# A written engine order for a decode step of attention and a gated MLP: q's copies first, softmax in front of GLU work, scores in two tiles

## Chip, cores, metric

The kernel runs on one core of one Trainium2 chip. The metric is the device time of one execution in microseconds (us). A profile's span is some 2.2 us shorter than the time of the same execution (81.6 against 83.79 in the profiled run of the kernel before). Some executions come out over 1.5% slower than the fastest of the same kernel; they are called slow, and only the other, fast runs are compared.

## The reference

One token, bf16. A 32-head attention with 8 key/value heads over the last 4096 positions of a cache, and a gated MLP of width 1792, mixed by a scalar gate g:

```python
q = (x @ wq)                                  # wq 512 x 4096
scores = einsum("bhqd,bhkd->bhqk", q, k) * Dh ** -0.5      # k, v: 8 heads x 4096 x 128
p = softmax(scores); o = einsum("bhqk,bhkd->bhqd", p, v)
a = o.reshape(1, 1, 4096) @ wo                # wo 4096 x 512
h = sigmoid(x @ w_gate) * (x @ w_up)          # 512 x 1792 each
b = h @ w_down
return g * a + (1 - g) * b                    # g = sigmoid(sum(x * gate_w))
```

Every weight and cache row is used once. The work is to move 30.67 MB and to keep the engines out of the way.

## The kernel before

One queue loads the weights and the cache in this order: wq, four pairs of key heads (kn), w_gate, w_up, four pairs of value heads (vv), w_down (wd), wo; the last pair of value heads comes in two halves, with half of wd behind each. The tile framework puts the instructions of an engine in an order of its own; the text below is not the order in which they ran. "PV" is the product of probabilities and values. In the code and the views qtT and qbig are q transposed and laid out as weights, kT the transposed keys, S_ps the scores, pm and hm their maxima, e_sb and eT the exponentials and their transpose, pv_ps the result of PV, a_ps the sum of the output row; `down()` adds rows of the product with wd to it.

```python
for k in range(8):                                   # q, broadcast over the partitions
    ...  nc.tensor.matmul(q_ps[:], lhsT=xT[...], rhs=wq_sb[:, c, ks], ...)
    nc.scalar.copy(q_sb[:, ks], q_ps[:])
    if k % 2: nc.vector.transpose(qtT..., q_sb...)
for qd in range(4):                                  # q into block-diagonal weights
    for t in range(2):
        nc.vector.tensor_copy(q_dst[rows, :, 32*qd:32*qd+R2, :, t], q_src[rows, :, :, :, 0, t])

S_ps = ps_S.tile([P, 4, 512], F32, name="S_ps", tag="S")        # one tile of 4 banks
for a in range(HP):                                  # 4 pairs of key heads
    for v in range(2):
        kT = ktp.tile(...); nc.vector.transpose(kT..., kn[a]...)
        ...  nc.tensor.matmul(S_ps[:, 2*v+hb, :], lhsT=q_st..., rhs=k_v..., start=False, ...)   # 8

for v in range(2): nc.vector.tensor_reduce(pm2[:, v:v+1], S_ps[:, 2*v:2*v+2, :]..., op=ALU.max)
nc.vector.tensor_tensor(pm[:], pm2[:, 0:1], pm2[:, 1:2], op=ALU.max)
...  # mt = pm^T (TensorE), hm = max over heads (VectorE), mb = hm^T (TensorE), nb (ScalarE)
for v in range(2):
    nc.scalar.activation(e_sb[:, v, :], S_ps..., AF.Exp, bias=nb[:], ..., accum_out=rs2[:, v:v+1])
    nc.vector.transpose(eT..., e_sb[:, v, :]...)
...  # GLU: gate and up products, sge = exp(-gate), sge+1, sg = 1/sge, h_sb, hT (VectorE)
...  # lsel, rb_ps, rb: 1/sum of the exponentials
for a in range(HP):
    for m in range(NP // 4):
        if a == HP - 1 and m == NP // 8: down(0, NJ_A)
        nc.tensor.matmul(pv_ps[32*a:32*a+32, :, :], lhsT=eT..., rhs=vv[a][:, 4*m:4*m+4, :], ...)
...  # o_ps, oT, oX, oY, the rest of down()
for c in range(NC_O):                                # wo, in six loads of 8, 8, 8, 5, 2, 1 chunks
    add_row(oY[:, c:c+1], wo_sb[:, c, :], False, c == NC_O - 1)      # two products of 256 columns
```

## Time and profile before

| | before |
|---|---|
| time, median of three runs | 84.48 us (84.08 to 84.76) |
| span of the profiled run | 81.6 us |
| TensorE / VectorE / ScalarE busy | 51.6 / 38.6 / 10.1 us |
| loads | 30.67 MB, 376 GB/s over the span |

In the page's rows of slices each digit is the busy share of one fortieth of the span in tenths (9 is 90% or more); PEclk is the clock granted to TensorE. In lines of chain and timeline the first number is the start in us, the second the length; a bracket at the end of a timeline line tells how long the engine stood idle before and what ended it. The prediction below shows these views.

### The profile page before, as it was taken

The numbers are of one execution on the slowest core, as the hardware profiler recorded it, in microseconds if no ns is written. First come the engines' busy times: TensorE is split into PE (matmuls) and PEld (weight loads), VectorE is DVE, ScalarE is ACT, GpSimd is POOL, SyncE is SP. The second block draws the span as 40 slices with busy tenths as digits, with TensorE's granted clock in tenths as the row PEclk, the third lists the DMA queues.
The fourth block names the chain that finished last, engine by engine and source line by source line (L and its number), as shares of the span: only waits on it lengthen the run. The fifth ranks groups of instructions, "written<-read, shape, count | busy, mean of one in ns | idle before, by whom it ended". The sixth has DMA issues, their size and how long they took to land.

```text
span 81.6 us, 791 instructions
## 1 busy us (share of the span) xinstructions
PE 51.6 (63%) x313; PEld 24.0 (29%) x313; DVE 38.6 (47%) x50; ACT 10.1 (12%) x18; POOL 3.3 (4%) x10
## 2 busy tenths in 40 slices
PE   0200286999400499999999063300999999967960
PEld 0200122344000233444443033000433444545830
DVE  0601820034999999999903995699300000002020
ACT  2300000376500000000000200910000000020010
POOL 7800000000000000000000000000000000000000
PEclk9999999999998555999999997555555999999999
DMA  5969969999999999999999999999999999995000
GB/s 161 353 289 482 514 273 490 393 418 474 401 426 458 410 434 425 436 422 412 421 422 458 410 426 450 409 426 391 417 428 420 420 422 422 424 399 217 0 0 1
DMA packets 3050, 30.71 MB, mean 376 GB/s; under 512 B 356, under 2 KB 616, under 8 KB 1128
## 3 DMA queue, kind: packets, MB, share of 16 engines
q1 hardware_dynamic: 3042, 30.67, 89.7%
q8 instruction: 2, 0.03, 0.2%
q10 hardware_dynamic: 6, 0.00, 0.0%
HBM read 30.67 MB, written 0.00 MB: 376 GB/s over the span
## 4 chain that ended last, share of the span: by engine, by line
PE 55%; DVE 24%; DMA 15%; ACT 1%; issue 1%
PE S_ps L215 20%; PE pv_ps L304 17%; DMA wq_sb<-in_A_wq_dram 15%; PE q_ps L184 8%; PE a_ps L290 6%; DVE kT L209 5%; DVE sg L266 4%; DVE pm L222 3%; DVE eT L242 3%; DVE h_sb L268 3%; DVE qbig L197 2%; DVE qtT L189 2%; PE o_ps L313 1%; PE gu_ps L255 1%; DVE hT L273 1%
## 5 line engine op out<-in xcount | busy, mean ns | idle before, releaser
L215 PE MATMUL S_ps<-kT,qbig 128*128 128x512 bf16 x64 | 16.6, 424 | 6.2 <-DVE qbig L197 6.2
L209 DVE STREAM_TRANSPOSE kT<-kn 128x2048 f32<-128x2048 f32 x8 | 17.8, 2275 | 0.0
L304 PE MATMUL pv_ps<-vv,eT 128*32 128x512 bf16 x64 | 14.2, 436 | 0.0
L215 PEld LDWEIGHTS <-qbig 128*128 128x128 bf16 x64 | 6.7, 106 | 16.1 <-DVE qbig L197 7.0
L184 PE MATMUL q_ps<-wq_sb,xT 128*128 128x512 bf16 x32 | 8.4, 428 | 1.0 <-DMA wq_sb<-in_A_wq_dram 1.0
L304 PEld LDWEIGHTS <-eT 128*32 128x32 bf16 x64 | 5.8, 109 | 7.6 <-issue 3.6
L315 DVE TENSOR_TENSOR oT<-o_ps,rb 128x32 bf16<-128x32 f32 x1 | 0.2, 191 | 15.2 <-PE o_ps L313 15.2
L189 DVE STREAM_TRANSPOSE qtT<-q_sb 128x512 f32<-128x512 f32 x4 | 2.8, 702 | 7.5 <-ACT q_sb L186 7.5
L203 PE MATMUL S_ps<-ident,other 2*128 2x512 bf16 x4 | 2.0, 611 | 5.8 <-DVE other L141 5.8
L186 ACT CAST q_sb<-q_ps 128x512 bf16<-128x512 f32 x8 | 4.7, 585 | 6.5 <-PE q_ps L184 6.5
L184 PEld LDWEIGHTS <-xT 128*128 128x128 bf16 x32 | 3.4, 108 | 6.4 <-issue 3.7
L279 PE MATMUL rb_ps<-lsel,ones_f 128*128 128x32 f32 x2 | 0.6, 398 | 5.6 <-DVE lsel L277 5.6
L222 DVE TENSOR_REDUCE pm<-S_ps 128x1 f32<-128x1024 f32 x2 | 2.4, 1219 | 3.2 <-PE S_ps L215 3.2
L290 PE MATMUL a_ps<-wo_sb,oY 128*1 128x256 bf16 x64 | 3.7, 272 | 0.0
L263 ACT ACTIVATE sge<-gu_ps 128x448 f32<-128x448 f32 x1 | 0.5, 543 | 23.1 <-PE gu_ps L258 23.1
L290 PEld LDWEIGHTS <-oY 128*1 128x1 bf16 x64 | 2.8, 84 | 0.7
L266 DVE RECIPROCAL sg<-sge 128x448 f32<-128x448 f32 x1 | 3.0, 2954 | 0.0
L309 ACT COPY pv_sb<-pv_ps 128x512 f32<-128x512 f32 x1 | 0.6, 586 | 18.7 <-PE pv_ps L304 18.7
L268 DVE SCALAR_TENSOR_TENSOR h_sb<-gu_ps,gg,sg 128x448 bf16<-128x448 f32 x1 | 2.2, 2154 | 1.5 <-PE gu_ps L255 1.5
L166 DVE TENSOR_TENSOR gpr<-xr 1x512 f32<-1x512 bf16 x1 | 0.7, 679 | 4.6 <-DMA xr<-in_gate_w_dram 4.6
L149 PE MATMUL xt_ps<-ident,xr 1*128 1x1 bf16 x4 | 0.3, 166 | 3.5 <-POOL ident L130 3.5
L203 PEld LDWEIGHTS <-other 2*128 2x128 bf16 x4 | 0.6, 158 | 6.2 <-DVE other L141 5.9
(60 smaller groups left out, 32.5 us busy)
## 6 DMA issues: line engine op xcount, KB each, us to landing
kn<-in_A_k_cache_dram SPq DMA_DIRECT2D x4, 2048.0 KB, 27.2
vv<-in_A_v_cache_dram SPq DMA_DIRECT2D x3, 2048.0 KB, 19.1
wq_sb<-in_A_wq_dram SPq DMA_DIRECT2D x1, 4096.0 KB
wo_sb<-in_A_wo_dram SPq DMA_DIRECT2D x3, 1024.0 KB, 22.9
vv<-in_A_v_cache_dram SPq DMA_DIRECT2D x2, 1024.0 KB
wg_sb<-in_B_w_gate_dram SPq DMA_DIRECT2D x1, 1792.0 KB, 32.9
wd_sb<-in_B_w_down_dram SPq DMA_DIRECT2D x2, 896.0 KB
wu_sb<-in_B_w_up_dram SPq DMA_DIRECT2D x1, 1568.0 KB
```

The source lines that it names most:

```text
L184: nc.tensor.matmul(q_ps[:], lhsT=xT[:, c:c + 1].to_broadcast([P, P]), rhs=wq_sb[:, c, ks], start=(c == 0), stop=(c == DC - 1))
L186: nc.scalar.copy(q_sb[:, ks], q_ps[:])
L189: nc.vector.transpose(qtT[:].bitcast(F32)[:, kq], q_sb[:].bitcast(F32)[:, kq])
L203: nc.tensor.matmul(S_ps[:, u, :], lhsT=other[:].rearrange("p o y u -> p (o y u)"), rhs=ident[0:2, 0:2].rearrange("p (o y) -> p o y", o=1). ...
L209: nc.vector.transpose(kT[:].bitcast(F32), kn[a][:, v * KB:(v + 1) * KB, :] .rearrange("p n d -> p (n d)").bitcast(F32))
L215: nc.tensor.matmul(S_ps[:, 2 * v + hb, :], lhsT=q_st[:, a, dhi, :, t], rhs=k_v[:, hb * 16:(hb + 1) * 16, dhi, :, t], start=False, stop=(a ...
L222: nc.vector.tensor_reduce(pm2[:, v:v + 1], S_ps[:, 2 * v:2 * v + 2, :].rearrange("p a b -> p (a b)"), axis=AX.X, op=ALU.max)
L242: nc.vector.transpose(eT[:, :, v * KB:(v + 1) * KB, :].rearrange("p a n r -> p n a r"), e_sb[:, v, :].rearrange("p (n a r) -> p n a r", a= ...
L266: nc.vector.reciprocal(sg[:], sge[:])
L268: nc.vector.scalar_tensor_tensor(h_sb[:].rearrange("p j i -> p i j"), gu_ps[1][:, 0:FQ].rearrange("p (i j) -> p i j", j=NJ), gg[:, 1:2], s ...
L290: nc.tensor.matmul(a_ps[32 * i:32 * i + 1, i, 0:HN], lhsT=lhsT, rhs=rhs[:, i * HN:(i + 1) * HN], start=start, stop=stop)
L304: nc.tensor.matmul(pv_ps[32 * a:32 * a + 32, :, :], lhsT=eT[:, a, 4 * m:4 * m + 4, :].rearrange("p n r -> p (n r)"), rhs=vv[a][:, 4 * m:4 ...
```

## The change

The intent is to shorten the compute chain, which ends last. From q on TensorE, VectorE and ScalarE run in the order of the text. (1) q's copies go in front of the second key transpose, and two of the eight go to ScalarE. (2) The softmax chain goes in front of the GLU's VectorE work, and the inverse sums leave the path to PV. (3) The scores get two tiles, so that the first maximum need not wait for the last product. The core of the diff:

```diff
+    ctx.enter_context(tc.manual_schedule(engines=ORDERED))     # TensorE, VectorE, ScalarE
+    S_ps = [ps_S.tile([P, 2, 512], F32, name="S_ps", tag="S") for _ in range(2)]
...
     for k in range(8):
...
+        if k == 1:
+            kTs[0, 0] = k_transpose(0, 0)
...
-            nc.vector.tensor_copy(q_dst[rows, :, 32 * qd:32 * qd + R2, :, t], q_src[rows, :, :, :, 0, t])
+            copy = nc.scalar.copy if qd == 3 else nc.vector.tensor_copy
+            copy(q_dst[rows, :, 32 * qd:32 * qd + R2, :, t], q_src[rows, :, :, :, 0, t])
...
-    S_ps = ps_S.tile([P, 4, 512], F32, name="S_ps", tag="S")
...
+    glu(0, wg_sb)                     # gate products behind the scores
+    sge = ...; nc.scalar.activation(sge[:], gu_ps[0][:, 0:FQ], AF.Exp, scale=-1.0)
     mt_ps = ...                       # mt, hm, mb, nb as before
+    glu(1, wu_sb)                     # up products beside the exponentials
     for v in range(2): ...            # exponentials, transposes
+    lsel = ...                        # then sge+1, reciprocal, h_sb, hT (moved here)
...
+        if a == 0:                    # rb behind the first quarter of PV
+            nc.tensor.matmul(rb_ps[:], lhsT=ones_f[:], rhs=lsel[:], start=True, stop=True)
```

## The prediction

> **What bounds the kernel now.** I read the page's row of slices first, then the chain that ended last, then that chain in order of time, and last the traffic of the loads near the end.
>
> The slices of the page of the kernel before (40 slices of 2.04 us each):
>
> ```profile
> PE   0200286999400499999999063300999999967960
> DVE  0601820034999999999903995699300000002020
> PEclk9999999999998555999999997555555999999999
> DMA  5969969999999999999999999999999999995000
> GB/s 161 353 289 482 514 273 490 393 418 474 401 426 458 410 434 425 436 422 412 421 422 458 410 426 450 409 426 391 417 428 420 420 422 422 424 399 217 0 0 1
> ```
>
> Two things run side by side. The loads are busy from the seventh slice to the 36th without a gap, at 390 to 490 GB/s. TensorE has two holes, one before the scores (slices 11 to 13) and one in the softmax (slices 22 to 28), and a half clock after each hole.
>
> The chain that ended last, in order of time (start, length, what):
>
> ```profile
> 0.73 12.16 DMA wq_sb<-in_A_wq_dram
> ...
> 25.95 0.32 DVE qbig L197 x2
> ...
> 27.56 16.58 PE S_ps L215 x64
> 44.14 0.02 issue
> 44.16 2.36 DVE pm L222 x2
> 46.52 0.30 DVE sge L264
> 46.82 0.07 DVE pm L225
> 46.89 2.92 DVE sg L266
> 49.81 0.14 DVE hm L229
> ...
> 57.30 0.61 PE rb_ps L279 x2
> 57.91 11.63 PE pv_ps L304 x52
> ...
> 74.47 4.40 PE a_ps L290 x78
> 78.87 0.40 DVE res L330
> ```
>
> So the end is set by compute: wq lands, q, key transposes in front of q's copies, scores 27.56 to 44.14, 13.8 us from there to the first PV product, 14 us of PV, tail. In the softmax, VectorE does the GLU's reciprocal (2.92 us) between the maximum and the step (hm) that TensorE waits for, and later h_sb (2.15) and hT (0.65) before the transposes of the exponentials.
>
> How near behind is the load stream? Windows of the kernel before near the end (last column GB/s, the one before it the load share):
>
> ```profile
> 74.50:75.00 0.50, 0.50 (x12) 0.40 (x10) 0.19 (x1) 0.00 (x0) 0.00 (x0) 1.00 0.62 221
> 75.00:75.50 0.50, 0.50 (x15) 0.39 (x12) 0.00 (x0) 0.00 (x0) 0.00 (x0) 1.00 0.15 49
> 75.50:76.00 0.50, 0.50 (x14) 0.41 (x10) 0.00 (x0) 0.00 (x0) 0.00 (x0) 1.00 0.00 0
> ```
>
> The last byte, the tail of wo, arrives at about 75.45 us of a span of 81.6. TensorE then still works through wo until 78.87, and from there to the end are 2.73 us. The output needs all of wo, so loads are a second bound, only about 3 us behind the first. **This is the number that decides the prediction.**
>
> **What the skill says.** "Perfetto Trace Analysis", Roofline, gives some 435 GB/s as what one core's 16 DMA engines can carry together; the trace agrees (421 to 435 GB/s over every stretch of several us from 12.9 to 72), so no order of compute can hurry the stream. "TensorE: Matmul & The Clock Gate", What's actually happening: after an idle window of about 3.4 us the clock halves, and a busy window of that length brings it back. The trace agrees: after each hole the clock row shows 5, and weight loads of the scores and of PV come 0.427 us apart at first, about 0.22 later. The same page, Architectural detail, says ScalarE and VectorE are strict first-in first-out. That is why a GLU reciprocal in the wrong place costs the chain its whole length, as seen above (hm starts at 49.81, the moment sg ends, though its product was ready near 47.4). "ScalarE: Activation LUTs", What ACT_TABLE_LOAD costs, gives 186 ns + 0.833 ns per element with immediate scale: 239 ns for the moved copies of 64 elements (an estimate from that page; the same formula gives 612 ns for the q copies of 512, where the trace has 585).
>
> **The change part by part.**
>
> 1. q's copies first. VectorE has now two key transposes (2.19 us each of chain) between qtT and qbig. One (0,0) moves into the wait for q: the first kn lands at about 17.7 (cumulated traffic of 4.19 + 2.10 MB), so it runs about 17.8 to 20.1. Then three qtT of 0.71; the last waits for the cast that ended at 21.95 and is done at about 22.7. Six copies instead of eight on VectorE at 1.77/8 = 0.22 each: 24.0. ScalarE does the other two beside them (2 x 0.24). Scores start at 24.0 instead of 27.56: **3.5 us earlier**.
>
> 2. Scores. Seven transposes remain from 24.0, at 2.21 us each back to back (13.28/6): last done at 39.5. Before, TensorE was the slower one here (64 products, the first dozen at half clock, 16.58 us). Now VectorE is: a block of 8 products takes 8 x 0.22 = 1.7 us at full clock. Last block ends at 39.5 + 1.75 = 41.3, so 2.85 us earlier than 44.14; 0.7 of the 3.5 are lost to VectorE.
>
> 3. Scores in two tiles. Before, the maximum of the first half waited for all 64 products (both reductions start after 44.14). Now the first (1.2 us) can run from 39.5 while the last block multiplies; only the second is exposed: 41.3 + 1.22 + 0.15 = 42.7. **1.2 us.**
>
> 4. Softmax chain in front of GLU work. TensorE: gate products (16 in 0.94 us) 41.3 to 42.3, hidden beside the second reduction; mt 0.3, hm 0.22 + 0.24, mb 0.58, nb 0.17, with gaps 44.4. Exponentials 1.1 each with an accumulator read: 45.7 and 46.8; transposes 1.13 each behind them: 46.8 and 47.95. The up products (0.95 us) hide behind the exponentials. rs and lsel 0.4 are no longer in front of PV, since the sum's product is written after the first quarter of PV. **PV starts at about 48.0 instead of 57.84: 9.8 us earlier in all.** add, reciprocal, h_sb, hT (0.38 + 2.95 + 2.15 + 0.65 = 6.1 us) end near 54.6, long before their first use.
>
> 5. PV then meets the data. By cumulated traffic the four vv land at about 45.7, 50.7, 55.5 and 62.6, wd's halves at 60.0 and 64.7, and wo's pieces at 67.2, 69.7, 72.8, 74.45, 75.1 and 75.45. PV from 48.0: 16 products are 3.4 us at full clock, 6.8 at half. With one slow start: 54, 57.6, 61, and the last half after 62.6 ends at 65.3. Copy, o_ps, oT, oX, oY take 2.4 us as before: wo could start at 68 and catches up with its second piece. About 2 us of slack remain against the stream, more because the small last pieces come late.
>
> 6. The end. Last wo piece: 75.45, plus 0.38 from last byte to first product (as wq: last byte near 12.56, product at 12.94) = 75.83. Waiting for pieces, TensorE is busy under half of the time (8 chunks warm = 0.9 of 2.45 us), so I expect half clock at the end. Then five chunks landing at 74.83 take 5 x 0.213 = 1.07, the next two 0.43, the last 0.21 with a drain: ends at 76.7. At full clock it is 76.2. Plus 2.73 from last product to end: span **78.95 (warm) to 79.45 (cold)**, against 81.6. The gain is 2.15 to 2.65 us, a quarter of the 9.8 us won on the compute chain.
>
> **Rivals.**
>
> A. No second bound in the way: the end moves with PV, 9.8 us earlier, some 74.7 us. Against it: wo's last byte at 75.45 and a stream already at its ceiling. The stream could end earlier only if it had waited for buffers; vv waits for key tiles, but the queue shows only 0.4 us of wait on the key transposes and no dip in the row, and the stream has deep work queued. I give this 2%.
>
> B. The written order stalls an engine: VectorE's early key transpose stands in front of three qtT, and a late kn would push q; or TensorE waits in gate, up or wd products in front of something ready. The loads of the GLU weights land by 41, before use; kn at 17.7 is close to the wish (17.5), so slips of 0.3 us are likely and cost nothing because part 5 has 2 us of slack. A stall of 4 us would bring "same": 83 to 84.5. 5%.
>
> C. The stream itself: the timed runs may load 1% slower than the profiled one. Before feels this only through wq (0.1 us), the new kernel feels all of it (0.75 us): 82.7. With that the verdict comes to the 2% line (82.79). This is the main way to "same".
>
> D. A colder end, with wo's earlier pieces also not caught up: at half clock each big piece takes 1.7 us, less than the 2.45 between landings, so the backlog is bounded, at most 0.5 us: 82.5.
>
> **Range.** From the median, 84.48 - 2.45 = 82.0 (before to after by spans, nearer the middle of warm and cold). C and D on one side, an overlap better by some 0.9 us on the other: 81.1 to 83.1. The line of 2% is 0.8 us above my value, against an uncertainty of about 0.6 in the middle: 0.83 faster, 0.16 same, 0.01 slower.
>
> **What will show it.** Scores begin near 24 and VectorE has no gap from 24 to 39.5; the first reduction overlaps the last products; hm directly follows mt; PV begins near 48; TensorE shows holes between wo products from 69 to 75.5 that end with wo's landing; the chain that ended last names the load of wo (or a queue of loads) instead of PV; traffic still stops near 75.4; last product to end still 2.7 us. I am wrong if traffic stops clearly earlier or later than 75.4, or if PV ends after 70, so that the compute chain stays the bound.

## The result

The changed kernel took 81.61 us (median of four fast runs, 81.31 to 82.08) against 84.41 us for the kernel before (84.08 to 84.76, four runs). The ratio is 0.967 with a 95% interval of 0.961 to 0.973. A ratio is the mean time of one kernel's fast runs over that of the other's fast runs of the same rounds, so it is not quite the ratio of the medians. Five further rounds on a chip used later gave 0.982 (0.974 to 0.990): the gain is 2 to 3%, and its size depends on something that the experiments come to.

The page of the changed kernel:

```profile
PE   0200194999914788898887547999998488724550
DVE  0601820029859999999986349999300000200020
PEclk9999999999999999999999995699999999999997
DMA  6789898999999999999999999999999999999600
GB/s 166 281 347 529 363 429 380 438 438 438 421 429 438 429 421 432 412 448 415 411 434 438 413 438 429 438 413 405 411 423 433 406 432 405 417 425 403 245 6 1
...
DMA 90%; SPq 4%; PE 2%; DVE 1%; issue 0%
DMA wg_sb<-in_B_w_gate_dram 42%; DMA vv<-in_A_v_cache_dram 25%; DMA wo_sb<-in_A_wo_dram 23%; SPq L85 3%; PE a_ps L300 2%; SPq L81 1%; DVE res L346 1%
```

The hole before the scores is short and the hole in the softmax nearly gone, yet TensorE is half idle or more near the end (slices 36 to 39). The loads run without a gap into the 38th slice (75.4 us), about as long as before. The chain that ended last is loads for 90% of the span. Before it was TensorE and VectorE.

The compute chain of the changed kernel, in order of time:

```profile
23.48 1.35 DVE L218 COPY qbig<-qtT 32x64 bf16<-32x64 bf16 x6
23.54 0.76 ACT L218 COPY qbig<-qtT 32x64 bf16<-32x64 bf16 x2 [0.84 <-DVE qtT L207]
24.84 1.89 PE L229 MATMUL S_ps<-kT,qbig 128*128 128x512 bf16 x8 [2.76 <-DVE qbig L218]
24.86 15.47 DVE L190 STREAM_TRANSPOSE kT<-kn 128x2048 f32<-128x2048 f32 x7
...
40.26 1.18 DVE L251 TENSOR_REDUCE pm<-S_ps 128x1 f32<-128x1024 f32 x1
...
42.32 1.23 DVE L251 TENSOR_REDUCE pm<-S_ps 128x1 f32<-128x1024 f32 x1 [0.88 <-PE S_ps L229]
...
44.30 0.28 DVE L260 TENSOR_REDUCE hm<-mt_ps 1x32 f32<-1x128 f32 x1 [0.56 <-PE mt_ps L258]
...
48.06 5.13 PE L315 MATMUL pv_ps<-vv,eT 128*32 128x512 bf16 x16 [1.43 <-DVE eT L274]
```

The scores start 2.7 us earlier than before, one reduction lies beside products, hm follows the maximum with no GLU work in between, and PV starts at 48.06 instead of 57.84. Then the products of wo, and the traffic near the end (last column GB/s):

```profile
68.77 1.04 PE L300 MATMUL a_ps<-wo_sb,oY 128*1 128x256 bf16 x16 [0.20 <-DMA wo_sb<-in_A_wo_dram]
71.26 1.04 PE L300 MATMUL a_ps<-wo_sb,oY 128*1 128x256 bf16 x16 [1.46 <-DMA wo_sb<-in_A_wo_dram]
73.75 1.04 PE L300 MATMUL a_ps<-wo_sb,oY 128*1 128x256 bf16 x16 [1.45 <-DMA wo_sb<-in_A_wo_dram]
75.33 1.26 PE L300 MATMUL a_ps<-wo_sb,oY 128*1 128x256 bf16 x16 [0.55 <-DMA wo_sb<-in_A_wo_dram]
```

```profile
75.00:75.50 0.50, 0.17 (x4) 0.14 (x5) 0.00 (x0) 0.00 (x0) 0.00 (x0) 1.00 0.19 68
75.50:76.00 0.50, 0.50 (x12) 0.30 (x10) 0.00 (x0) 0.00 (x0) 0.00 (x0) 1.00 0.05 16
```

Each of the three big pieces of wo is waited for and used up before the next is there; the products of the three small ones (the last line) run together. The last packet of wo's last piece (the only 128 packets of 1024 bytes in that stretch) ends at 75.84 us, where the kernel before had it at 75.45. The last product ends at 76.60, and 2.78 us later the span is over.

### The profile page after: what moved, and what is told of

The parts are those of the page before. It is cut to its first block, busy times and chain, and to the rows that moved or that the text cites. A ratio compares the mean times of both kernels' runs of the same rounds, so it can differ in the third digit from the quotient of the medians.

```text
span 79.4 us, 799 instructions
## 1 busy us (share of the span) xinstructions
PE 52.4 (66%) x313; PEld 23.2 (29%) x313; DVE 38.6 (49%) x48; ACT 10.9 (14%) x20; POOL 3.3 (4%) x10
## 4 chain that ended last, share of the span: by engine, by line
DMA 90%; SPq 4%; PE 2%; DVE 1%; issue 0%
DMA wg_sb<-in_B_w_gate_dram 42%; DMA vv<-in_A_v_cache_dram 25%; DMA wo_sb<-in_A_wo_dram 23%; SPq L85 3%; PE a_ps L300 2%; SPq L81 1%; DVE res L346 1%
## 5 line engine op out<-in xcount | busy, mean ns | idle before, releaser
L229 PE MATMUL S_ps<-kT,qbig 128*128 128x512 bf16 x64 | 15.2, 377 | 5.0 <-DVE qbig L218 2.8
L315 PE MATMUL pv_ps<-vv,eT 128*32 128x512 bf16 x64 | 14.8, 408 | 2.9 <-DMA vv<-in_A_v_cache_dram 1.5
L229 PEld LDWEIGHTS <-qbig 128*128 128x128 bf16 x64 | 6.1, 97 | 14.1 <-issue 4.2
L202 PE MATMUL q_ps<-wq_sb,xT 128*128 128x512 bf16 x32 | 9.0, 451 | 1.4 <-DMA wq_sb<-in_A_wq_dram 1.4
L300 PE MATMUL a_ps<-wo_sb,oY 128*1 128x256 bf16 x64 | 4.4, 272 | 3.6 <-DMA wo_sb<-in_A_wo_dram 3.6
L274 DVE STREAM_TRANSPOSE eT<-e_sb 128x1024 bf16<-128x1024 bf16 x2 | 2.4, 1224 | 1.9 <-ACT e_sb L272 1.9
L300 PE MATMUL a_ps<-wd_sb,hT 128*1 128x256 bf16 x28 | 2.2, 271 | 0.6 <-DMA wd_sb<-in_B_w_down_dram 0.6
```

What stands on the lines that cost most here:

```text
L202: nc.tensor.matmul(q_ps[:], lhsT=xT[:, c:c + 1].to_broadcast([P, P]), rhs=wq_sb[:, c, ks], start=(c == 0), stop=(c == DC - 1))
L229: nc.tensor.matmul(S_ps[v][:, hb, :], lhsT=q_st[:, a, dhi, :, t], rhs=k_v[:, hb * 16:(hb + 1) * 16, dhi, :, t], start=False, stop=(a == HP ...
L274: nc.vector.transpose(eT[:, :, v * KB:(v + 1) * KB, :].rearrange("p a n r -> p n a r"), e_sb[:, v, :].rearrange("p (n a r) -> p n a r", a= ...
L300: nc.tensor.matmul(a_ps[32 * i:32 * i + 1, i, 0:HN], lhsT=lhsT, rhs=rhs[:, i * HN:(i + 1) * HN], start=start, stop=stop)
L315: nc.tensor.matmul(pv_ps[32 * a:32 * a + 32, :, :], lhsT=eT[:, a, 4 * m:4 * m + 4, :].rearrange("p n r -> p (n r)"), rhs=vv[a][:, 4 * m:4 ...
```

## The experiments

A call is a set of runs on one chip. All outputs passed the comparison with the reference. Two kernels compute a wrong result on purpose and passed as well, so the comparison is too coarse to see that part of wo; it says nothing of their correctness.

### Half of wo, in both kernels

The first pair asks which kernel the loads bind: 2.1 MB less to load, the same products.

```diff
-    WO_SPLIT = (0, 8, 16, 24, 29, 31, 32)
+    WO_SPLIT = (0, 8, 13, 15, 16)
-        add_row(oY[:, c:c + 1], wo_sb[:, c, :], False, c == NC_O - 1)
+        add_row(oY[:, c:c + 1], wo_sb[:, c % 16, :], False, c == NC_O - 1)
```

In the kernel before:

> The kernel before with only half of wo loaded, each loaded piece used twice (wrong result on purpose): 2.1 MB less, the same products. Theory (before, the compute chain set the end): the stream ends near 70.5 us instead of 75.45, and the span stays at 81.6 +- 0.4. Rival (the stream bound the kernel before too): the span falls by up to 4.9 us.

In the changed kernel:

> The changed kernel with the same half of wo (wrong result on purpose). Theory (the last byte of wo sets the end): the stream ends near 71 us; TensorE has oY near 68.5 and 64 products of wo left, half of which wait for nothing after the stream's end, so the last product is near 73.1 and the span near 75.9, 3.5 us less than 79.4. Rival (the changed kernel is still bound by PV): span stays at 79.4 within 0.5.

Before: ratio 0.998 (0.989 to 1.007), span 81.5, though its last byte came at 70.68, 4.8 us earlier. Changed: ratio to the kernel before 0.934 (0.928 to 0.939), span 76.1, last byte at 70.84. The products of wo, first of the kernel before with half of wo, then of the changed kernel with half of wo:

```profile
75.12 3.66 PE L290 MATMUL a_ps<-wo_sb,oY 128*1 128x256 bf16 x64
```

```profile
70.33 3.01 PE L300 MATMUL a_ps<-wo_sb,oY 128*1 128x256 bf16 x48 [0.54 <-DMA wo_sb<-in_A_wo_dram]
```

The same cut is worth nothing before and 3.3 us after (spans of 79.4 and 76.1; the whole changed kernel had not run in this call, and the ratio fell from 0.967 in the first result to 0.934). So the bound changed from compute to the stream: shown, not only argued.

### A longer softmax chain

The second pair asks how far ahead of the stream the compute chain runs. One reciprocal, or three, are put between the maximum and hm:

```diff
     glu(0, wg_sb)
+    for _ in range(1):                      # 3 in the second kernel
+        nc.vector.reciprocal(pad[:], pad[:])     # 128 x 448, result unused
```

> The changed kernel with one more VectorE reciprocal of 128x448 (2.95 us) between the maximum and hm, in the middle of the softmax chain, its result unused. It lengthens the chain by about 2.4 us (VectorE idles 0.56 there already): PV starts near 50.5. Theory (PV runs ahead of the data by about 5.7 us, summed from TensorE's waits for vv, wd and wo): span unchanged, 79.4 +- 0.4. Rival (chain still bounds the end): 81.8.

> The same with three of the reciprocals: the chain is 8.3 us longer, PV starts near 56.4. Theory: some 5.7 us are swallowed by the slack, the rest shows: span about 82, between 81.3 and 83.5, depending on the granted clock after a longer hole. Rival (chain still bounds): 87.7. Rival (much more slack than I count): 79.4.

The profiled run with one was slow; its three fast runs had a mean of 81.83 us, ratio 0.978 (0.970 to 0.985), on a chip where the changed kernel itself had not run. Again beside the changed kernel:

> The changed kernel itself, as the anchor for the other three of this call on one chip. Span 79.4 to 80.9: the last byte of wo came at 75.5 to 76.7 us in the runs so far, whatever the compute did, and the span is that plus 3.5 to 4.2.

> delay_1 again beside its anchor, since its profiled run was of the slow state and its fast runs lay 1% over what I expected from another chip. Theory (2.5 us longer softmax chain lies in the slack): same as the anchor within 0.5 us, TensorE still waits for wo's pieces. Rival (part of the chain's length reaches the end): 1 to 2.4 us slower than the anchor.

The changed kernel as anchor had 82.23 us (mean of five fast runs, 81.72 to 82.85) and a span of 79.9; with one reciprocal 81.69 us (six, 81.35 to 81.88), span 79.9. With one reciprocal:

```profile
50.06 5.32 PE L319 MATMUL pv_ps<-vv,eT 128*32 128x512 bf16 x16 [0.31 <-DVE eT L278]
...
73.64 3.45 PE L304 MATMUL a_ps<-wo_sb,oY 128*1 128x256 bf16 x32 [1.46 <-DMA wo_sb<-in_A_wo_dram]
```

PV starts 1.5 us later than in the anchor of the same chip (48.52; I had expected 2.4, but its q was quicker) and TensorE still waits 1.46 us for a piece of wo: the time has not grown. With three, PV starts at 56.7, and no product of wo waits for anything:

```profile
74.74 3.66 PE L304 MATMUL a_ps<-wo_sb,oY 128*1 128x256 bf16 x64
```

Its span is 81.5, ratio 1.002 (0.995 to 1.010). A chain 8.6 us longer (56.7 against 48.06) ends 1.8 us later (78.40 against 76.60), so some 6.8 us were swallowed; I had counted 5.7. The two profiles are of different calls.

### Each part alone

If the end is a floor at the stream, any part that shortens the chain by over some 2 us should reach it. Part 2 alone puts back parts 1 and 3:

```diff
-        if k == 1:
+        if k == 5:
             kTs[0, 0] = k_transpose(0, 0)
+    kTs[0, 1] = k_transpose(0, 1)
-            copy = nc.scalar.copy if qd == 3 else nc.vector.tensor_copy
-            copy(q_dst...
+            nc.vector.tensor_copy(q_dst...
-    S_ps = [ps_S.tile([P, 2, 512], ...) for _ in range(2)]
+    S_all = ps_S.tile([P, 4, 512], F32, name="S_ps", tag="S")
```

> The changed kernel with the softmax chain in front of the GLU work, but q's copies behind two key transposes and all on VectorE as before, and the scores in one tile as before. Chain: scores end near 44.2, PV starts near 51 instead of 48. Theory (stream bounds, 5.7 us of slack): span 79.4, the same as the whole change within 0.4, so this part alone is worth all of the gain. Rival (every part adds to the end): about 81.6 - 2.3*0.6 = 80.2 or later.

Measured: ratio 0.975 (0.968 to 0.982), between the two values of the whole change; span 79.6. The kernel with part 2 alone:

```profile
51.72 6.42 PE L316 MATMUL pv_ps<-vv,eT 128*32 128x512 bf16 x16 [1.43 <-DVE eT L275]
...
75.55 1.27 PE L301 MATMUL a_ps<-wo_sb,oY 128*1 128x256 bf16 x16 [0.53 <-DMA wo_sb<-in_A_wo_dram]
```

PV starts 3.7 us later than with the whole change and the end is the same, with wo waited for. No gain of parts 1 and 3 on top of part 2 shows within the intervals.

Part 1 alone, and none of the three:

> The changed kernel with q's copies first alone: the GLU's add, reciprocal, h_sb and hT are put back in front of hm and of the exponentials' transposes, the sum's product in front of PV, the scores in one tile. Chain: scores end near 42.2, PV starts near 56, about 2 us earlier than the kernel before. Theory: the end moves with the chain until it meets the stream: span 79.4 to 79.9, since 81.6 - 2 is just at the stream's 79.4. Rival (only the softmax order matters): 81.6.

> All three parts put back, only the written order itself kept (the kernel before's order written down by hand, as its trace shows it). Both theories: span 81.6 +- 0.5, PV from 57.8: same as before. If it differs, something of the change that I do not name (the written order itself) moves the time.

Both came out slower than I expected: 0.983 (0.974 to 0.991) and 1.012 (1.002 to 1.022). I had written the old softmax order down wrongly: the up products stood behind mb, and from the end of the scores to PV it took 15.5 us in both kernels, where the kernel before took 13.7. So the second is no control for the written order itself, and what that order is worth alone stays untested. Against each other the two do say something: the ratio with part 1 is lower by 0.03, from three fast runs of each (three of the first kernel's six runs were slow). PV starts at 57.90 in the one and at 60.73 in the other, but this second profile is of a slow run. With the up products back in front of hm:

```diff
+    glu(1, wu_sb)
     hm = work.tile([1, 4, HQ], F32, name="hm")
...
-    glu(1, wu_sb)
     h_sb = work.tile([P, NJ, 32], BF16, name="h_sb")
```

> q's copies first alone, now with the up products in front of the second small softmax product as the kernel before ran them (my first version had them behind it and its softmax took 15.5 us instead of 13.7). PV starts near 56, so the chain alone would end near 79.0. Theory: end at the stream's floor, within 0.5 us of the anchor. Rival (the softmax order is needed): 1 us or more slower than the anchor.

Measured: ratio 0.971 (0.964 to 0.977), mean of five fast runs 81.27 us (81.00 to 81.43), span 79.3. **This is 1.0 us less than the whole change on the same chip** (82.23, of which the fastest run is 81.72), and it beats both kernels. My rival, that the softmax order is needed, falls; but a gain over the anchor I had not expected either. PV and the last wo products of this kernel, and then those last products of the anchor:

```profile
54.94 10.98 PE L317 MATMUL pv_ps<-vv,eT 128*32 128x512 bf16 x53
...
75.24 1.26 PE L299 MATMUL a_ps<-wo_sb,oY 128*1 128x256 bf16 x16 [0.54 <-DMA wo_sb<-in_A_wo_dram]
```

```profile
73.56 3.58 PE L300 MATMUL a_ps<-wo_sb,oY 128*1 128x256 bf16 x32 [1.45 <-DMA wo_sb<-in_A_wo_dram]
```

The windows of the last 8.5 us (TensorE busy first, then weight loads and the other engines; the third last column is the granted clock), of part 1 alone and of the anchor:

```profile
69.00:72.00 3.00, 2.79 (x35) 2.00 (x37) 0.59 (x3) 0.00 (x0) 0.00 (x0) 1.00 1.01 414
72.00:75.00 3.00, 1.98 (x34) 1.30 (x29) 0.00 (x0) 0.00 (x0) 0.00 (x0) 1.00 0.84 330
```

```profile
69.00:72.00 3.00, 1.56 (x28) 1.05 (x25) 0.00 (x0) 0.00 (x0) 0.00 (x0) 1.00 1.00 415
72.00:75.00 3.00, 1.55 (x18) 0.88 (x15) 0.00 (x0) 0.00 (x0) 0.00 (x0) 0.59 0.86 341
```

And of the whole change in its first profile, that of the result above:

```profile
69.00:72.00 3.00, 1.54 (x30) 1.12 (x26) 0.00 (x0) 0.00 (x0) 0.00 (x0) 1.00 1.00 414
72.00:75.00 3.00, 1.34 (x22) 0.78 (x19) 0.00 (x0) 0.00 (x0) 0.00 (x0) 1.00 0.87 342
```

The stream's last byte came at 75.73 in part 1 alone and at 75.63 in the anchor. From there to the last product it took 0.77 us in the one, at full clock, and 1.51 us in the other, at half clock. The anchor's TensorE had run ahead, stood idle half of the time while it waited for wo, and had lost its clock when the last pieces came. The kernel that starts PV 6.4 us later has hardly any idle time from 69 to 72. But the first profile of the whole change was as idle as the anchor and kept its clock: an idle TensorE can lose it there and need not. That this pair of profiles differs by clock at the end is shown; that the 1.0 us between the timed runs has this cause alone is not, since a run's record has only its mean clock.

On this chip the mean times of the fast runs were, by the start of PV in the profile: 82.23 us (48.5, the anchor), 81.69 (50.1, one reciprocal), 81.65 (51.7, part 2 alone), 81.27 (54.9, part 1 alone), 82.27 (57.9, its first version, in which no product of wo waited). So the earliest PV was not the fastest. The profile of the kernel with one reciprocal has half clock at the end as well (1.36 us from last byte to last product) and the anchor's span, 79.9; what its other, faster runs had at their end is not on record.

### The load of w_up

In the traces sixteen packets are in flight, each followed by the next, so the packets can be put in order into sixteen chains (a reconstruction: the trace does not name the engines). In the changed kernel they end between 73.9 and 75.84 us. The kernel loads the end of w_up in four small loads; I took these for the cause:

```diff
-    dq.dma_start(wu_sb[...][:, 0:LM], ...)      # main part
-    ... dq.dma_start(wx_sb[32 * b:32 * b + 32, h, :], wx_v[h, b])      # 4 loads
+    dq.dma_start(wu_sb[:], B_w_up.rearrange("(p c) f -> p c f", c=DC))
```

> The changed kernel with w_up loaded whole over 128 partitions, in place of a main part and four small loads of 32 partitions. In the traces of both kernels eight of sixteen packet chains carry all the 1792-byte packets, and the chains end between 73.9 and 75.8 us. Theory (the stream's end is set by the most loaded chains): spread evenly, the last byte comes near 75.1 instead of 75.84, the span near 78.7. Rival (the spread at the end has another cause): last byte and span unchanged, 75.8 and 79.4.

It fell. Ratio 0.981 (0.975 to 0.988), no better than the anchor's 0.982; last byte at 76.51. Fourteen chains ended within 0.4 us (74.23 to 74.59), and two late, at 75.95 and 76.51. Two loads of 16 KB on a queue named instruction stood near 39.3 and 65.9 us. At the first, one chain had no packet for 1.1 us and then one of 1.00 instead of 0.54 us. A kernel with fewer TensorE instructions should have one less:

```diff
-        for i in range(2):
-            nc.tensor.matmul(a_ps[32 * i:32 * i + 1, i, 0:HN], lhsT=lhsT, rhs=rhs[:, i * HN:(i + 1) * HN], ...)
+        nc.tensor.matmul(a_ps[0:1, 0, 0:N_OUT], lhsT=lhsT, rhs=rhs, ...)
```

> even_wu with 501 instead of 601 TensorE instructions (rows of wd and wo as one product of 512 columns instead of two of 256, no products for the extra x). In even_wu two loads of the queue named instruction, 16 KB each, near 39 and 66 us, each held one of the sixteen packet chains for 1.1 us, and two chains ended at 76.0 and 76.5 where the other fourteen ended near 74.5. Theory (an instruction load for every 256 instructions of TensorE holds one DMA engine back): one such load instead of two, one late chain instead of two. The end is still set by that one: last byte near 76.2, span 79.5 to 80.3. Rival (the two late chains have another cause): still two late chains, with one load of instructions.

Inconclusive: the kernel still had two of these loads, as the row of its queues says, and two late chains (75.91 and 76.04):

```profile
q8 instruction: 2, 0.03, 0.2%
```

I had taken too few instructions away. The trace has 538 rows of TensorE, control rows included, instead of 634 (I had counted 501 and 601), and in all fourteen profiles the second load comes when TensorE has begun 429 to 472 rows. Ratio 0.982 (0.977 to 0.988), which says little either: the edit also changed the copy and store of the output, and eight chunks of wo took TensorE 1.89 us in it, as eight products, against 1.04 us as sixteen in the other kernels. That late chains and instruction loads belong together fits all of this and is not shown by a kernel with one load. It stays open.

## Why the prediction was right

**The deciding number held.** I put the second bound at the last byte of wo, 75.45 us, and the span 3.5 to 4 us behind it. Measured: 75.84, and 3.54 us. My sign of being wrong, traffic that stops clearly later than 75.4, was 0.4 us off here and up to 1.2 us in the fast profiles of its variants. Time 81.61 against 82.0 predicted. Rival A (the end moves with PV, 9.8 us) is refuted by half of wo and by the reciprocals: most of the 9.8 us won on the chain lies in waits for vv and wo.

**Part by part.** Scores start: 24.84, not 24.0. q took 9.00 us instead of 8.40, its first products at half rate for longer (0.43 us apart, though the PEclk row shows 9 there), and the two copies on ScalarE took about 0.5 us each, not the 0.24 from the page's formula; they still ended before VectorE's (24.30 against 24.83). Scores bound by VectorE: right, seven transposes in 15.47 us without a gap, and TensorE idle 0.3 us in front of each block. First reduction hidden: right (40.26, beside the products that start at 40.39). PV at 48.06, predicted 48.0, but by two errors that cancel: the chain ran 1 us late, and PV did not wait for the second transpose of the exponentials (it starts inside the pair's 46.76 to 49.13), which I had put in front of it. In reading the rows I had put the second hole at slices 22 to 28; it is 23 to 28.

**The slack of step 5 was too small.** I had about 2 us between the chain and the stream. The waits of TensorE in the first profile sum to 5.7 us, and the three reciprocals found some 6.8. So rival B's size was wrong too: PV 3.7 us later (part 2 alone) did not bring "same" but 0.975. One term of it shows in the traces: the pieces are there later than cumulated traffic says. Products that waited for the last vv, and for the second and third piece of wo, started at 63.88, 71.26 and 73.75 us, where I had 62.6, 69.7 and 72.8 for the data.

**Step 6 was right in range and wrong in its choice.** I expected half clock at the end. The first profile had full clock there (PEclk 1.00 from 75 to 76) and 0.76 us from last byte to last product; the anchor had half clock and 1.51 us. I had put 0.5 us between the cases; it was 0.75. In the first profile the full clock and a last byte 0.39 us later than before made up for each other.

**Rival C** (a slower stream reaches the new kernel whole) was the right worry, though not by a slower rate. The last byte came anywhere from 75.45 to 76.61 us in the fast profiles that loaded all of wo, which the kernel before did not feel. The rate of the whole stream hardly differed (29.6 of the 30.7 MB had come by 72.1 to 72.3 us in all of them); the late chains did.

**What I missed:** that the parts are not additive, and that a later PV could be better. After the floor is reached, more haste bought nothing here; in the anchor it left TensorE idle before it lost its clock.

## What to carry to other kernels

Before a chain is shortened, find where the next bound ends (here the last byte plus its tail); that, not the chain, sizes the gain, and one part of the change may be enough to get it. Test it by taking bytes away and by adding delay: a bound answers to one and not to the other. And when TensorE waits for the last pieces of a stream, its clock there is part of the tail (0.77 or 1.51 us here): a schedule that is only just early enough, as part 1 alone here, can beat one that is far ahead, though why it did by 1.0 us is not settled.

## What the Trainium skill lacked or had wrong

- "TensorE: Matmul & The Clock Gate", What's actually happening: the table gives the half clock after an idle window; no share of busy time at which it is lost is given on the page. Here it also came after windows that were far from idle: in the anchor TensorE was busy for 44% of the 3.41 us ahead of the loss at 72.6 us, in the kernel before for 42% ahead of that at 49.8. No clean share came out of it: with part 2 alone a window with 62% (47.2 to 50.6 us) lost the clock and one with 45% (71.1 to 74.5) kept it.
- "Runtime: NRT & Kernel Launch", Instruction fetch mechanics: it calls the cost of crossing a 16 KiB block mostly hidden. In the kernel with w_up loaded whole, which the load stream binds, two instruction loads of 16 KB were in the stream, each 1.1 us long, and fifteen packets instead of sixteen were in flight meanwhile (during the first load one chain got its next packet at 40.37 us, where its turn was near 39.3). What that costs at the end is open.
- "ScalarE: Activation LUTs", What ACT_TABLE_LOAD costs: the formula, which the page gives for a tile of 128 partitions, makes 239 ns of 64 elements. The two strided copies of 32x64 bf16 took 472 and 555 ns; the copies of 128x512 from PSUM took 586 ns where it gives 612.
